# Expert 0's first chunk: low parts on GpSimd from a copy in SBUF, and a routing group's temporaries moved to PSUM

## The chip, the core and the metric

The kernel runs on one core of a Trainium2 chip. The metric is the device time of one execution in microseconds (us). A core has five instruction queues that matter here: PE (the matrix unit TensorE), DVE (VectorE), ACT (ScalarE), POOL (GpSimd) and SP (SyncE, which here only issues transfers). Each works through its own instructions in order and waits on semaphores for the others.

## The reference, cut to what matters

A linear attention with a decaying state makes `x` (3072 tokens of 384 numbers), and a mixture of 8 experts with two chosen per token works on it:

```python
logits = x @ w_gate
noise_scale = np.log1p(np.exp(x @ w_noise))
noisy_logits = logits + noise_scale * noise
top2 = np.argpartition(-noisy_logits, 2, axis=1)[:, :2]
...
for e in range(E):
    for k in range(2):
        mask = top2[:, k] == e
        h = np.maximum(x[mask] @ w1[e], 0.0)
        out[mask] += top2_w[mask, k, None] * (h @ w2[e])
```

`w1[e]` is 384 by 1024, `w2[e]` is 1024 by 384, everything is float32.

## The kernel before, in words

**Attention, then experts.** The tokens come in 24 blocks of 128. A loop over the blocks does the attention, stores each block of `x` to a scratch array `xd` in device memory, and computes the logits. The blocks form two routing groups, 0 to 11 and 12 to 23. When a group's logits are there, `route(g)` finds the two best experts of each token, counts with matmuls how many earlier tokens chose the same expert, and so gives each token a place in its expert's list. `drop` makes 0/1 matrices out of the places, and `place` multiplies them on PE, so that the token numbers land at their places in a list `L`. `rows` turns `L` into row numbers `GR`, and POOL gathers the rows from `xd` by indirect transfers (`xgather`).

**Experts in chunks.** An expert has up to 832 tokens, in a chunk of 3 tiles of 128 tokens and a chunk of 3 such tiles and one of 64. `p1(e, ci)` is the first product of a chunk: for each of 8 blocks `f` of the hidden size it makes a PSUM tile `ph` with 9 matmuls. `p2(e, ci)` is the second product: for each tile of tokens 24 matmuls into a PSUM tile `pym`. Both split every float32 factor into a high part (rounded to fp32r, a shorter format) and a low part (the rest), and add three products: high by high, high by low, low by high. So behind each `ph` the activations are needed twice: ACT writes the high part of `relu(ph)` into `hb[:, f, 0]`, and DVE writes `max(ph, 0)` minus the high part into `hb[:, f, 1]`. `p2` takes the blocks `f` in order, and of each the high part twice and then the low part.

**Routing among the products.** Group 0 is routed while the attention runs. Group 1 is complete only when the attention ends, and the whole of the list for expert 0's second chunk depends on it. So its `route(1)` is a generator, of which `rstep` takes some steps at each point of `p1(0, 0)` (after each of the 8 blocks, each time with a credit of `STEPS_P1`) and of `p2(0, 0)` (every fourth matmul). The instructions of both stand mixed in DVE's queue in that order. Two points bind PE to it. The counting matmuls (L842 to L848, into the PSUM bank `RT`) need the one-hot matrix `r_om` of DVE (L834). And `place` (L728) needs the 0/1 matrices, which DVE makes (L706, L711, L714) and ACT scales (L719). A finished `drop` waits in `late_mm` with a count of steps, 2, until its matmuls are issued.

**Temporaries.** In group 0 `route` keeps its temporaries in free columns of the PSUM bank `RT` (`own` is true); in group 1 it keeps them in `PS`, a tile in SBUF. In the first case the gates are stored to `xd` by the branch at L870 to L890, in the second by that at L899 to L908.

**Buffers.** `stg` is a pool of 3 SBUF tiles through which the weights come in. Expert 0's weights are split before `p1(0, 0)`; expert 1's first loads go through `stg` after `p2(0, 0)`.

Of the kernel before, what the change touches and what calls it, by code (L numbers as in the profile page):

```python
# [9 lines left out]
F32 = mybir.dt.float32  # L10
# [5 lines left out]
AF = mybir.ActivationFunctionType  # L16
# [13 lines left out]
FILL = 1  # L30
PVB = 4
CV_EARLY = 3
STEPS_P1 = 1.15
STEPS_P2 = 4.2
STEPS_R = 1.6
STEPS_L0 = 0.9
# [21 lines left out]
def kernel(  # L58
# [14 lines left out]
    nc = tc.nc  # L73
    B, H, S, D = r.shape
    N, E = noise.shape
# [18 lines left out]
    NJ = NM + 1  # L94
    XW = DM + E
    GROUPS = ((0, 12), (12, 24))
    GB = max(b - a for a, b in GROUPS)
# [517 lines left out]


    RT = psum.tile([128, 512], F32, name="RT", tag="rt")
    PS = rtp[0].tile([128, 4 * GB * E], F32, name="PS", bufs=1)
    PG = [RT]

    def P(k, shape):
# [66 lines left out]
    def drop(g, mm2, ej2, ijv, w_, c0, first):  # L688

        i0, i1 = GROUPS[g]  # L690
        wp_ = w_ + w_ % 2
        o = 5 * GB * E + E
        o = o if o + 2 * wp_ <= 512 else 0
        pL = RT[:, o:o + 2 * wp_].rearrange("p (a b) -> p a b", a=2)
        c = 0.1 + 0.004 * wp_
        n = GD
        parts = []
        while late_mm:
            yield "hold"
        for j0 in range(0, i1 - i0, n):  # L700
            js = slice(j0, j0 + n)
            oa = rtp[0].tile([128, n, 128], BF16, name="r_oa", bufs=2)
            ob = rtp[0].tile([128, n, 2 * E * NJ], BF16, name="r_ob", bufs=2)[:, :, :2 * wp_].rearrange(
                "p n (a b) -> p n a b", a=2)
            sh = [128, n, 64, 2]
            nc.vector.tensor_tensor(oa.rearrange("p n (a b) -> p n a b", b=2), mm2[:, js, None, :].to_broadcast(sh),  # L706
                                    im[:, None].to_broadcast(sh), op=ALU.is_equal)
            yield 0.45
            sh = [128, n, wp_ // 2, 2]
            o0, o1 = (ob[:, :, a].rearrange("p n (a b) -> p n a b", b=2) for a in range(2))  # L710
            nc.vector.tensor_tensor(o1, ej2[:, js, None, :].to_broadcast(sh),  # L711
                                    ijv.rearrange("p (a b) -> p a b", b=2)[:, None].to_broadcast(sh), op=ALU.is_equal)
            yield c
            nc.vector.tensor_mul(o0, o1, thi[:, i0 + j0:i0 + j0 + n, None, :].to_broadcast(sh))  # L714
            yield c
            parts.append((oa, ob))
            yield 0.05
        late_mm.append([2, lambda: place(n, parts, pL),
                        lambda: [nc.scalar.activation(ob[:, :, 1], ob[:, :, 1], AF.Copy, scale=pcol) for _, ob in parts],  # L719
                        lambda: placed(pL, w_, c0, first), False])  # L720

    late_mm = []

    def place(n, parts, pL):
        m = len(parts) * n
        for j in range(m):
            oa, ob = parts[j // n]
            nc.tensor.matmul(pL.rearrange("p a b -> p (a b)"), oa[:, j % n, :],  # L728
                             ob[:, j % n].rearrange("p a b -> p (a b)"), start=(j == 0), stop=(j == m - 1))
# [20 lines left out]
    def route(g, lists=True, behind=iter(())):  # L750
        i0, i1 = GROUPS[g]
        n = i1 - i0
# [2 lines left out]
        sh = [128, n, E]  # L755
        T = T_of(n)

        PG[0] = PS if lists and g == len(GROUPS) - 1 else RT
        if g:
            while lists and late_mm and g < len(GROUPS) - 1:  # L760
                yield "hold"
# [405 lines left out]
    def p1(e, ci, mid=lambda: None):  # L1167
# [8 lines left out]
        for f in range(NF):  # L1176
# [8 lines left out]
            for j, (a, x, d) in enumerate(q):  # L1185
                nc.tensor.matmul(ph[:, :w_], a[:, d, fs], x[:, d, :w_], start=(j == 0), stop=(j == len(q) - 1))  # L1186
                if j == 4:
                    mid()
            for h_, a, b in parts:
                nc.scalar.activation(h_[:, f, 0, :], ph[:, a:b], AF.Relu)  # L1190
            for h_, a, b in parts:
# [334 lines left out]
    for s in range(1, len(seq)):  # L1526
        e, ci = seq[s]
# [188 lines left out]
```

## Time and profile before

| what | value |
|---|---|
| runs, median of 3 | 588.56 us (586.28 to 589.39) |
| profiled execution, its own time | 585.73 us |
| its span, first to last instruction | 583.7 us |
| PE busy | 565.8 us, 97% of the span |
| DVE, ACT, POOL busy | 343.4, 283.9, 281.2 us |
| mean granted clock of TensorE | 0.998 of full speed |

The span is a little shorter than the execution's own time, which also holds what lies before the first and behind the last instruction. The median of the runs is 2.83 us above the profiled execution. Durations below come from that one execution.

### The profile page before, as it was taken

Reading aid. Unit: us, or ns where it says so; the run is one execution under the profiler, and the core shown is the slowest. Engines: PE = TensorE matmul, PEld = TensorE weight load, DVE = VectorE, ACT = ScalarE, POOL = GpSimd, SP = SyncE. Lnnn points to the kernel's source line nnn. Section 1 sums busy time; section 2 is a strip of 40 time slices with the busy share of each in tenths; the row PEclk is TensorE's granted clock in tenths of the full one; section 3 lists DMA queues with packets and bytes.
Section 4 is the critical chain, followed back from the end, with each engine's and each line's share of the span. In section 5 each row is a group of like instructions: output and inputs, shape, how many; then the busy total and the mean of one; then the engine's idle time right before and its main releaser. Section 6 shows DMA issues by size and latency. Waiting matters only on the chain.

```text
span 583.7 us, 13848 instructions
## 1 busy us (share of the span) xinstructions
PE 565.8 (97%) x5351; PEld 540.9 (93%) x5352; DVE 343.4 (59%) x788; ACT 283.9 (49%) x714; POOL 281.2 (48%) x420
## 2 busy tenths in 40 slices
PE   8999898999999999999999999999999999999995
PEld 5899897989989999999999999999999999999995
DVE  7898796898772744545455554545363556454331
ACT  4348786842553525455444554544545455445220
POOL 8998776911445532354433453535162455333322
PEclk9999999999999999999999999999999999999999
DMA  8988998476515725566456738455646556433111
GB/s 162 200 196 189 221 233 196 130 210 192 156 34 177 230 88 148 156 155 188 111 179 101 189 101 204 135 166 152 142 128 144 167 134 179 111 97 99 54 35 42
DMA packets 143289, 86.53 MB, mean 148 GB/s; under 512 B 118688, under 2 KB 133279, under 8 KB 143216
## 3 DMA queue, kind: packets, MB, share of 16 engines
q1 hardware_dynamic: 132432, 56.76, 40.4%
q0 software_dynamic: 10160, 28.81, 16.6%
q8 instruction: 44, 0.72, 0.5%
q14 instruction: 29, 0.24, 0.1%
q10 hardware_dynamic: 624, 0.00, 0.1%
HBM read 58.81 MB, written 19.86 MB: 135 GB/s over the span
## 4 chain that ended last, share of the span: by engine, by line
PE 84%; POOL 5%; DMA 3%; DVE 2%; issue 2%; SPq 2%; ACT 1%; POOLq 0%; DVEq 0%; ACTq 0%
PE ph L1186 37%; PE pym L1222 34%; PE py L535 3%; DMA kt<-in_k_dram 3%; PE pym L1215 2%; PE pym L1213 2%; POOL rku L414 2%; POOL kd L406 2%; PE PAB L480 2%; SPq L158 1%; POOL rku L418 1%; PE KX L228 1%; PE py L577 1%; PE py L437 1%; PE RT L728 1%
## 5 line engine op out<-in xcount | busy, mean ns | idle before, releaser
L1222 PE MATMUL pym<-w1h,hb 128*128 128x384 f32 x768 | 200.4, 337 | 0.0
L1222 PEld LDWEIGHTS pym<-w1h,hb 128*128 128x128 f32 x768 | 139.4, 188 | 0.2
L1192 DVE SCALAR_TENSOR_TENSOR hb<-ph,hb 128x384 fp32r<-128x384 f32 x128 | 71.0, 556 | 115.4 <-ACT ht L1190 74.5
L1186 PE MATMUL ph<-xh,w0h 128*128 128x384 f32 (+1 forms) x384 | 135.5, 353 | 0.0
L1186 PE MATMUL ph<-xh,w0l 128*128 128x384 f32 (+1 forms) x384 | 135.2, 352 | 0.0
L1186 PE MATMUL ph<-xl,w0h 128*128 128x384 f32 (+1 forms) x384 | 129.9, 352 | 0.0
L1222 PE MATMUL pym<-w1l,hb 128*128 128x384 f32 x384 | 129.3, 337 | 0.0
L1190 ACT ACTIVATE hb<-ph 128x384 fp32r<-128x384 f32 x128 | 62.7, 491 | 105.1 <-PE ph L1186 102.2
L1247 POOL DMA_INDIRECT out_dram<-ot,TK x56 | 60.5, 1081 | 100.1 <-DVE ot L1241 42.8
L1075 POOL DMA_INDIRECT xg<-xd,GR x56 | 60.1, 1073 | 48.7 <-DVE r_e L611 25.3
L1186 PEld LDWEIGHTS ph<-xh,w0h 128*128 128x128 f32 x384 | 72.2, 188 | 3.7 <-issue 0.2
L1186 PEld LDWEIGHTS ph<-xh,w0l 128*128 128x128 f32 x384 | 72.2, 188 | 3.1
L1186 PEld LDWEIGHTS ph<-xl,w0h 128*128 128x128 f32 x384 | 71.9, 188 | 3.3
L1090 POOL DMA_INDIRECT pv<-out_dram,GA x49 | 50.4, 1028 | 51.0 <-DMA out_dram<-ot,TK 38.6
L1222 PEld LDWEIGHTS pym<-w1l,hb 128*128 128x128 f32 x384 | 72.2, 188 | 0.1
L1160 ACT ACTIVATE xh<-xj 128x384 fp32r<-128x384 f32 (+1 forms) x42 | 21.1, 502 | 43.4 <-DVE xj L1158 43.2
L1230 ACT ACTIVATE ot<-pym 128x384 f32<-128x384 f32 x42 | 20.4, 486 | 39.7 <-PE pym L1222 32.8
L1161 DVE TENSOR_TENSOR xl<-xj,xh 128x384 fp32r<-128x384 f32 (+1 forms) x42 | 22.5, 535 | 24.8 <-ACT xh L1160 24.8
L1146 ACT ACTIVATE pl<-xg 128x768 uint16<-128x768 uint16 (+1 forms) x42 | 35.3, 841 | 2.8 <-DMA xd<-pl 2.8
L488 DVE TENSOR_TENSOR am<-PAB,mneg 128x512 int32<-128x512 int32 x48 | 30.8, 684 | 3.7 <-PE PAB L480 3.2
L457 ACT ACTIVATE cv<-vt,c 128x48 f32<-128x48 f32 x120 | 30.2, 324 | 0.2
L406 POOL TENSOR_TENSOR kd<-kt,tabk 128x192 f32<-128x192 f32 x46 | 28.3, 635 | 3.9 <-DMA kt<-in_k_dram 3.5
(309 smaller groups left out, 821.2 us busy)
## 6 DMA issues: line engine op xcount, KB each, us to landing
stg<-in_moe_w_dram SPq DMA_DIRECT2D x24, 512.0 KB, 4.7
stg<-in_moe_w_dram SPq DMA_DIRECT2D x32, 384.0 KB, 3.7
xd<-x SPq DMA_DIRECT2D x24, 196.0 KB, 3.2
rd<-in_r_dram SPq DMA_DIRECT2D x24, 192.0 KB, 4.3
vt<-in_v_dram SPq DMA_DIRECT2D x24, 192.0 KB, 3.7
out_dram<-ot SPq DMA_DIRECT2D x16, 288.0 KB, 4.2
kt<-in_k_dram SPq DMA_DIRECT2D x23, 192.0 KB, 4.2
xg<-xd,GR POOLq DMA_INDIRECT x56, 3.1
```

Source lines behind the costliest of these rows:

```text
L406: nc.gpsimd.tensor_mul(KD[i][:, h], kt[i][:, h], tabk[:, h, :D])
L457: nc.scalar.activation(CV[i][:, h, :], vt[i][:, h, :], AF.Copy, scale=C8[i][:, h, :])
L488: nc.vector.tensor_tensor(am[:, :, h].bitcast(I32), pa[:, :, h].bitcast(I32), mneg[:, None].to_broadcast([128, 2, NP // 2, 128]), op=ALU.b ...
L1075: nc.gpsimd.indirect_dma_start(out=xg[:n, :XW if e else DM], out_offset=None, in_=xd[:rows_of(early_)], in_offset=bass.IndirectOffsetOnAxi ...
L1090: nc.gpsimd.indirect_dma_start(out=pv[:n], out_offset=None, in_=out, in_offset=bass.IndirectOffsetOnAxis(ap=GA[:n, e * NJ + t:e * NJ + t + ...
L1146: nc.scalar.activation(pl[:n], XG[e, t][:n, :DM].bitcast(U16).rearrange("p (d two) -> p two d", two=2), AF.Copy)
L1161: nc.vector.tensor_sub(xl, xj, xh.bitcast(F32))
L1186: nc.tensor.matmul(ph[:, :w_], a[:, d, fs], x[:, d, :w_], start=(j == 0), stop=(j == len(q) - 1))
L1190: nc.scalar.activation(h_[:, f, 0, :], ph[:, a:b], AF.Relu)
L1192: nc.vector.scalar_tensor_tensor(h_[:, f, 1, :], ph[:, a:b], 0.0, h_[:, f, 0, :].bitcast(F32), op0=ALU.max, op1=ALU.subtract)
L1222: nc.tensor.matmul(py, hb[:, f, a, hs], x[:, f, :], start=(j == 0), stop=(j == len(q) - 1))
L1247: st = nc.gpsimd.indirect_dma_start(out=out, out_offset=bass.IndirectOffsetOnAxis(ap=TK[:n, q:q + 1], axis=0), in_=ot[:n], in_offset=None, ...
```

## The change

Four edits. In `p1` of the first chunk of expert 0 only, ACT writes `relu(ph)` as float32 into a tile of the pool `stg` (L1189 of the changed kernel), a second ACT instruction rounds this copy into the high part, and POOL, no longer DVE, subtracts to get the low part. Group 1's temporaries lie in the columns of `RT`, as group 0's do, and `PS` is gone. `STEPS_P1` is 1.65 in place of 1.15. And the first list of group 1 waits 3 steps in place of 2 before its `place` is issued.

```diff
-STEPS_P1 = 1.15
+STEPS_P1 = 1.65
...
-    PS = rtp[0].tile([128, 4 * GB * E], F32, name="PS", bufs=1)
...
-        late_mm.append([2, lambda: place(n, parts, pL),
+        late_mm.append([3 if first is False and w_ == NJ else 2, lambda: place(n, parts, pL),
...
-        PG[0] = PS if lists and g == len(GROUPS) - 1 else RT
...
+            if (e, ci) == seq[0]:
+                ht32 = stg.tile([128, 1024], F32, name="stg")[:, :wb]
+                nc.scalar.activation(ht32, ph[:, :wb], AF.Relu)
+                nc.scalar.activation(hb[:, f, 0, :], ht32, AF.Copy)
+                nc.gpsimd.tensor_sub(hb[:, f, 1, :], ht32, hb[:, f, 0, :].bitcast(F32))
+                yield
+                continue
```

Line numbers of the changed kernel differ: from `P` to `route` they are 1 less, from there to `p1` 2 less, and behind the new lines 5 more.

The first place is PE in `p1(0, 0)`, where the counting matmuls of group 1 start. Before, they stand behind the last of the 72 matmuls into `ph`:

```order
L1186 MATMUL ph<-xh,w0h_891 128x384
L1186 MATMUL ph<-xl,w0h_891 128x384
L1186 MATMUL ph<-xh,w0l_892 128x384
L842 LDWEIGHTS ltri
L842 MATMUL RT<-r_om,ltri 128x96 [waits DVE_49]
L844 LDWEIGHTS ones_b
L844 MATMUL RT<-r_om,ones_b 128x88
```

In the changed kernel these rows stand behind the 54th matmul into `ph`, that is behind block 5 of 0 to 7:

```order
L1184 MATMUL ph<-xh,w0h_890 128x384
L1184 MATMUL ph<-xl,w0h_890 128x384
L1184 MATMUL ph<-xh,w0l_891 128x384
L840 LDWEIGHTS ltri
L840 MATMUL RT<-r_om,ltri 128x96 [waits DVE_49]
L842 LDWEIGHTS ones_b
L842 MATMUL RT<-r_om,ones_b 128x88
```

The 13 counting matmuls and their wait for DVE moved 18 matmuls forward.

The second place is PE at the first list's `place` in `p2(0, 0)`. Before, it stands behind the 20th matmul into `pym`:

```order
L1222 MATMUL pym<-w1h_1660,hb 128x384
L1222 MATMUL pym<-w1h_1660,hb 128x384 [waits Activation_49]
L1222 MATMUL pym<-w1l_1661,hb 128x384
L728 LDWEIGHTS r_oa [waits DVE_49]
L728 MATMUL RT<-r_ob,r_oa 128x16 [waits Activation_49]
L728 LDWEIGHTS r_oa
L728 MATMUL RT<-r_ob,r_oa 128x16
```

In the changed kernel it stands behind the 8th, and the low parts before it wait for POOL:

```order
L1227 MATMUL pym<-w1h_1659,hb 128x384 [waits Pool_49]
L1227 MATMUL pym<-w1h_1659,hb 128x384
L1227 MATMUL pym<-w1l_1660,hb 128x384
L727 LDWEIGHTS r_oa [waits DVE_49]
L727 MATMUL RT<-r_ob,r_oa 128x16 [waits Activation_49]
L727 LDWEIGHTS r_oa
L727 MATMUL RT<-r_ob,r_oa 128x16
```

`place` moved 12 matmuls forward within `p2`.

The third place is DVE in the middle of `p1(0, 0)`, in `route(1)`. Before, the low parts (L1192) stand among the routing steps:

```order
L779 RECIPROCAL r1r<-PS 128x96 [waits DVE_49]
L781 TENSOR_TENSOR r_s<-r_nl,r1r 128x96 [waits DVE_49]
L783 TENSOR_TENSOR r_s_3033<-r_s 128x96 [waits DVE_49]
L784 SCALAR_TENSOR_TENSOR r_sn<-r_s,nz 128x96
L1192 SCALAR_TENSOR_TENSOR hb<-ph,hb 128x384 [waits Activation_49]
L786 TENSOR_SCALAR PS<-r_s_3033 128x96 [waits DVE_49]
```

In the changed kernel they are gone from DVE, and `RT` stands for `PS`:

```order
L777 RECIPROCAL RT<-RT 128x96 [waits DVE_49]
L779 TENSOR_TENSOR r_s<-r_nl,RT 128x96 [waits DVE_49]
L781 TENSOR_TENSOR r_s_3019<-r_s 128x96 [waits DVE_49]
L782 SCALAR_TENSOR_TENSOR r_sn<-r_s,nz 128x96
L784 TENSOR_SCALAR RT<-r_s_3019 128x96 [waits DVE_49]
```

DVE loses 8 such instructions, 6 of them ahead of `r_om`, and POOL has 8 new ones, in front of the four gathers of the list that `place` fills.

## Rows read from the trace of the kernel before

**Rows 1.** The page's chain that ended last: shares by engine, then by line.

```profile
PE 84%; POOL 5%; DMA 3%; DVE 2%; issue 2%; SPq 2%; ACT 1%; POOLq 0%; DVEq 0%; ACTq 0%
```

**Rows 2.** Stretches: length; busy us (xcount) of PE, PEld, DVE, ACT, POOL; clock; DMA.

```profile
124.60:137.60 13.00, 13.00 (x83) 12.85 (x82) 12.24 (x46) 3.71 (x9) 0.00 (x0) 1.00 0.99 303
137.60:143.00 5.40, 4.49 (x45) 4.18 (x42) 4.45 (x24) 1.08 (x3) 0.00 (x0) 1.00 0.48 156
```

**Rows 3.** PE's instructions in order of time: start us, duration us.

```profile
124.86 0.34 PE L1186 MATMUL ph<-xh,w0l 128*128 128x384 f32 x1
...
137.15 0.33 PE L1186 MATMUL ph<-xh,w0l 128*128 128x384 f32 x1
137.32 0.22 PE L842 MATMUL RT<-r_om,ltri 128*128 128x96 bf16 x1
...
137.76 0.42 PE L1222 MATMUL pym<-w1h,hb 128*128 128x384 f32 x1
...
141.96 0.29 PE L728 MATMUL RT<-r_ob,r_oa 128*128 128x16 bf16 x6 [0.43 <-ACT r_ob L719]
142.74 0.29 PE L728 MATMUL RT<-r_ob,r_oa 128*128 128x16 bf16 x6 [0.49 <-ACT r_ob L719]
```

**Rows 4.** PE, the same view, at a later list's matmuls in `p1(0, 1)`.

```profile
161.18 0.36 PE L1186 MATMUL ph<-xl,w0h 128*128 128x448 f32 x1
161.64 0.86 PE L728 MATMUL RT<-r_ob,r_oa 128*128 128x100 bf16 x12
```

**Rows 5.** DVE's instructions in order of time, in `p1(0, 0)` and behind it.

```profile
125.39 0.25 DVE L763 SCALAR_TENSOR_TENSOR PS<-lg 128x96 f32<-128x96 f32 x1
125.92 0.26 DVE L766 SCALAR_TENSOR_TENSOR PS<-lg,nz 128x96 f32<-128x96 f32 x1
...
136.12 0.55 DVE L1192 SCALAR_TENSOR_TENSOR hb<-ph,hb 128x384 fp32r<-128x384 f32 x1
136.59 0.16 DVE L827 TENSOR_SCALAR r_da<-r_da 128x12 f32<-128x12 f32 x1
136.66 0.20 DVE L834 TENSOR_TENSOR r_om<-OH 128x96 bf16<-128x96 bf16 x1
...
138.51 0.16 DVE L599 TENSOR_SCALAR r2t<-r_da 128x12 f32<-128x12 f32 x1
...
142.14 0.18 DVE L714 TENSOR_TENSOR r_ob<-r_ob,thi 128x48 bf16<-128x48 bf16 x1
```

**Rows 6.** Groups of instructions with their shapes: busy us, mean ns of one, idle before.

```profile
L599 DVE TENSOR_SCALAR PS<-r_a 128x96 f32<-128x96 f32 x1 | 0.2, 204 | 0.0
L599 DVE TENSOR_SCALAR RT<-r_a 128x96 f32<-128x96 f32 x1 | 0.3, 260 | 0.0
...
L358 POOL TENSOR_TENSOR w1l<-stg,w1h 128x384 fp32r<-128x384 f32 x2 | 2.0, 1008 | 0.0
...
L1190 ACT ACTIVATE hb<-ph 128x384 fp32r<-128x384 f32 x128 | 62.7, 491 | 105.1 <-PE ph L1186 102.2 <-DVE mx L1057 1.9 <-DVE PS L611 1.0
...
L1160 ACT ACTIVATE xh<-xj 128x384 fp32r<-128x384 f32 x36 | 18.9, 525 | 32.0 <-DVE xj L1158 31.9
...
L719 ACT ACTIVATE r_ob<-r_ob,pcol 128x48 bf16<-128x48 bf16 x4 | 1.2, 326 | 4.0 <-DVE r_ob L714 4.0
```

**Rows 7.** DVE in order of time, in the attention, while POOL computes.

```profile
72.04 0.82 DVE L766 SCALAR_TENSOR_TENSOR RT<-lg,nz 128x96 f32<-128x96 f32 x1
...
113.35 0.52 DVE L940 TENSOR_SCALAR GR<-lt 128x3 int32<-128x3 f32 x1
```

**Rows 8.** POOL in order of time, at the same two moments, and its gathers after `p1(0, 0)`.

```profile
72.01 1.42 POOL L425 TENSOR_TENSOR rku<-rT,kT 128x256 f32<-128x256 f32 x2 [1.35 <-DVE r_a L765]
...
112.70 1.15 POOL L414 TENSOR_TENSOR rku<-rd,kt 128x192 f32<-128x192 f32 x2
...
144.12 0.94 POOL L1075 DMA_INDIRECT xg<-xd,GR  x1 [25.33 <-DVE r_e L611]
```

**Rows 9.** Later execution of the same DVE line, with POOL idle.

```profile
143.68 0.17 DVE L940 TENSOR_SCALAR GR<-lt 128x4 int32<-128x4 f32 x1
```

## The prediction

> **What bounds the kernel now.** First the chain that ended last: PE is 84% of it [rows 1], and PE is busy 565.8 of the 583.7 us of the span, so time can only come from the few places where PE stands still. The change touches the stretch from 124.6 us on, where expert 0's first products begin, so I read the busy time by stretch next. In the first product PE works all 13.00 us, DVE 12.24 of them, POOL none. Right behind it PE works only 4.49 of 5.40 us [rows 2]. PE's own order of time shows where: in front of the two halves of the list's `place` it waits 0.43 and 0.49 us for ACT's scaling [rows 3], together 0.92 us. The same kind of wait returns twice, smaller, in `p1(0, 1)`: the matmul at 161.18 should be followed after some 0.20 us, and the `place` begins at 161.64 [rows 4], so 0.26 us; its second half waits some 0.16 more by the same reading, and the other one (at 168.17) is alike. That is 2 x 0.42 = 0.84 us. All waits of PE on the routing of group 1 are thus 0.92 + 0.84 = **1.76 us**, and the change can win no more than that: everything else in this stretch is matmuls, whose number it doesn't alter. The counting matmuls cost no wait before: the last `ph` matmul starts at 137.15, they at 137.32, the first of `p2` at 137.76 [rows 3].
>
> **The change, part by part.** I work out when each of the two meeting points of PE and DVE comes now.
>
> *PE's side of the comparison.* The 72 matmuls into `ph` go from 124.86 (the second) to 137.15, that is 12.29 us for 70 steps, 0.1756 us each [rows 3]. The counting matmuls now stand behind the 54th, so PE asks for `r_om` at 124.86 + 53 x 0.1756 = 134.17 us.
>
> *DVE's side.* Before, `route(1)` starts at 125.39 and `r_om` is done at 136.66 + 0.20 = 136.86 [rows 5]. Six of the eight low parts lay ahead of it. The last of them starts at 136.12 and the next instruction at 136.59, 0.47 us later [rows 5]; since they overlap with the end of the one before, I take 0.37 each, 2.2 us for six (2.8 at 0.47). That gives 134.66. The temporaries in PSUM cost a little: the same instruction took 260 ns on `RT` and 204 ns on `PS` [rows 6]; some seven of the chain are of this kind, 0.35 us. So `r_om` comes at about 135.0 us (134.4 to 135.0 by the two values for a low part), and PE, which waited nowhere here, now **waits 0.85 us** (0.25 to 0.85). The steps were sped up by more than DVE was relieved. Queued behind that wait on PE are the last 18 matmuls of the first product and all of `p2`.
>
> *The port.* POOL was idle here [rows 2]; now it subtracts 8 times. A subtraction of this shape took 1008 ns on POOL [rows 6], and one comes every 9 x 0.1756 = 1.58 us, so POOL is busy 64% of the time. The trace shows what that does to DVE: L766, which reads `lg` and `nz`, both in SBUF, took 0.26 us with POOL idle (at 125.92) [rows 5], but 0.82 us at 72.04 [rows 7], while the first of two POOL multiplications of 0.71 us each ran from 72.01 [rows 8]. And L940 took 0.52 us at 113.35 [rows 7], beside the second half of 1.15 us of POOL work from 112.70 [rows 8], and 0.17 us with POOL idle [rows 9]. DVE ends when POOL's instruction ends. The Trainium skill ("SBUF — State Buffer", section "Who interferes with whom") says it as a rule: a DVE instruction with two SBUF inputs (or one in a two-port mode, which single-input ones can have) and a GpSimd instruction that reads SBUF exclude each other, and the one that comes second waits for the whole of the other; the trace agrees with its 0.82 us. By that rule the move of the temporaries takes most of `route(1)` out of reach, and only a few instructions are left.
>
> Those with both inputs in SBUF are, ahead of `r_om`, L783 with L784 and L816 (squares, noise, the difference of the maxima), and behind it L857, two L706 and two L714. Each may lose nothing or up to 1.0 us. Block k's subtraction begins when PE's nine matmuls, ACT's relu of 491 ns and ACT's copy of 525 ns [rows 6] are done: the third (k = 2) ends on PE at 124.86 + 26 x 0.1756 = 129.4, so it runs from about 130.7 to 131.7. L783 comes by my chain at 130.9, into it: 0.7 us late. L816 then comes at 135.3, between two subtractions. I take 0.65 of the 0 to 2.0 us that the two could lose together, so the wait at the comparison becomes **1.5 us** in all (0.25 to 2.85).
>
> *The place.* From the end of the counting matmuls, PE has 18 x 0.1756 + 8 x 0.1756 = 4.57 us of matmuls up to `place`, and some 0.25 more to its second half. DVE needed from L599 at 138.51 to the end of the second L714 at 142.14 + 0.18, 3.81 us [rows 5], then ACT, which is now behind relu and copy of block 7 (3.16 + 0.49 + 0.53 + two scalings of 326 ns that overlap a little [rows 6]: 4.8 us). Without the port PE would wait for nothing. With it, the first L714 comes (at 2.95) during block 6's subtraction (2.7 to 3.7) and the second (at 4.5) during block 7's (4.3 to 5.3): ACT is done at some 5.9, a wait of 1.1 us. I take **1.0 us**, near the upper end, since the trace shows the port at work (0 to 1.3), against 0.92 before.
>
> *The later lists.* The one issued in the middle of a block of `p1(0, 1)` keeps its 0.42 us, since ACT has just got that block's relu in front of the scalings. The three others stand between tiles; by the same sums they lose 0 to 0.3 each. I take 0.64, against 0.84.
>
> *What costs nothing.* ACT's 8 copies (525 ns [rows 6]) lie under PE's 1.58 us a block; ACT was busy 3.71 of 13.00 us [rows 2]. The last low part, 5.3 us behind the counting matmuls at the latest, is used by PE at 18 + 8 + 15 matmuls, 7.2 us, plus the `place`: 2 us to spare; without this cover each block's subtraction would cost its 1.0 us. POOL's queue: the four gathers of the second chunk stand behind the 8 subtractions. They began at 144.12 after 25.33 us of idling [rows 8], and will begin within 1 us of that, since `place` comes at the same time by the sums above; the subtractions are over by some 142. The loads of expert 1's weights on SP wait for the last subtractions in `stg`, and are issued long after. The gates' store of the other branch still stands on SP behind the same 16 zero stores and waits for the gathers.
>
> *Sum.* 1.5 (new wait) + (1.0 - 0.92) + (0.64 - 0.84) = **+1.4 us**. From there to the end PE works without a gap that could take it in. Against the profiled 585.73 us that makes 587.1; against the median of the runs, which is 2.83 us above it, 588.56 + 1.4 = **590.0 us**.
>
> **The rivals.**
>
> *The steps fit: a gain.* DVE's relief could be larger than 0.37 a low part and the two-input instructions fall between subtractions. Then the comparison waits 0.25, the place 0, and the later lists 0.42: 0.67 against 1.76, so -1.1 us, 587.5. For it: DVE 12.24 of 13.00 busy [rows 2], so it was the limit of the routing. Against it: PE asks 137.32 - 134.17 = 3.15 us earlier, `r_om` had 0.46 to spare [rows 3, 5], and six low parts give back 2.2.
>
> *The port decides: slower by more than 0.5%.* Both exposed instructions ahead of `r_om` lose a whole subtraction (0.85 + 2.0 = 2.85), and the five behind it hold the place up by 2.0: 2.85 + (2.0 - 0.92) - 0.2 = +3.7 us, 592.3. It decides from 3.2 us of blocking in all. For it: DVE's 0.82 us [rows 7]. Against it: with POOL at 64%, half a subtraction is what a blocked one loses on average. By the rule of the Trainium skill ("SBUF — State Buffer", above) blocks of these sizes happen, as in my forecast; it would not by itself make all seven whole.
>
> *The change moves the wait and nothing else.* Without any effect of the port the comparison waits 0.85, the place 0, the later lists 0.64: 1.49 against 1.76, -0.3 us, 588.3.
>
> **How the numbers follow.** Chances: my forecast 0.50 (its own range, with the port's two terms at nothing and at their largest short of the rival, 588.3 to 592), wait moved only 0.20, gain 0.16, port decides 0.10, something else late, POOL's low parts for instance, 0.04. Three runs of before lie 3.1 us apart, about 0.5%, which is what a measurement of this kernel can tell from no change; so the forecast, the moved wait and the gain all lie inside 0.5% (2.9 us), and even the whole 1.76 us would. Faster by over 0.5%: 0.05, for the runs' scatter; slower: 0.12, from the port and the rest; the same: 0.83. The range runs from the gain less half a microsecond of scatter, 587.0, to the port's rival, 592.3.
>
> **What will show it.** In the changed profile: a wait of PE in front of the counting matmuls for DVE of 0.25 to 2.9 us (none: the DVE sum is wrong); DVE's L783, L816 and L714 at 0.3 to 1 us, far above the 0.26 of such an instruction with POOL idle (unchanged: the port is no term); the wait at `place` about as long as before or gone; POOL's subtractions at about 1.0 us; the gathers within 1 us of 144. The forecast would be wrong if POOL's subtractions took over 1.58 us each, so that they fall behind PE, or if a transfer of the second chunk came late for PE's transposes.

## The result, and the profile after

The changed kernel takes 593.91 us (median of 13 runs, 590.62 to 596.48), the kernel before 586.49 in 13 runs on the same chip: a ratio of 1.0112 [1.0091, 1.0133]. That is slower by more than 0.5%, 1.6 us above the upper end of the predicted range. An execution more than 1.5% above the fastest of its kernel counts as slow, and all ratios here are of the others, while the medians hold every execution. The profiled execution has a span of 588.9 us (its own time 590.62) against 583.7 (585.73).

The chain that ended last, shares by engine; DVE had 2% before [rows 1]:

```profile
PE 83%; DVE 6%; SPq 3%; POOL 3%; DMA 2%; issue 2%; ACT 1%; POOLq 0%; DVEq 0%; ACTq 0%
```

PE in order of time (start us, duration us; in brackets the idle time before the instruction and what ended it), where [rows 3, 4] stood:

```profile
125.55 0.44 PE L1184 MATMUL ph<-xh,w0h 128*128 128x384 f32 x1
...
134.99 0.34 PE L1184 MATMUL ph<-xh,w0l 128*128 128x384 f32 x1
137.48 0.20 PE L840 MATMUL RT<-r_om,ltri 128*128 128x96 bf16 x1 [2.15 <-DVE RT L835]
...
139.24 0.52 PE L1184 MATMUL ph<-xh,w0h 128*128 128x384 f32 x1
...
142.69 0.34 PE L1227 MATMUL pym<-w1h,hb 128*128 128x384 f32 x1
...
144.27 0.52 PE L727 MATMUL RT<-r_ob,r_oa 128*128 128x16 bf16 x12
...
159.33 0.47 PE L1184 MATMUL ph<-xh,w0h 128*128 128x448 f32 x1 [0.42 <-ACT xh L1103]
...
161.47 0.43 PE L727 MATMUL RT<-r_ob,r_oa 128*128 128x100 bf16 x6 [0.59 <-ACT r_ob L718]
```

PE waits 2.15 us for the counts, and not for `r_om` (L830) but for the line behind it, L835. The `place` at 144.27 waits for nothing. The matmul at 139.24 takes 0.52 us where that at 134.99 took 0.34. The stretches around it say why (busy us of PE, PEld, DVE, ACT, POOL; granted clock; DMA share; GB/s):

```profile
135.00:137.40 2.40, 0.33 (x2) 0.10 (x2) 2.12 (x10) 1.01 (x2) 1.81 (x2) 1.00 0.93 295
137.40:139.00 1.60, 1.52 (x20) 1.52 (x20) 0.84 (x8) 0.00 (x0) 0.14 (x1) 0.93 1.00 317
139.00:142.00 3.00, 3.00 (x11) 3.00 (x10) 2.72 (x14) 1.01 (x2) 0.38 (x1) 0.50 0.79 254
142.00:143.00 1.00, 1.00 (x6) 1.00 (x6) 0.93 (x4) 0.05 (x1) 0.62 (x1) 0.90 0.00 0
```

After the idle gap PE came back and was granted 0.50 of its clock (1.2 instead of 2.4 GHz) for about 3 us, though it was busy throughout. The 18 matmuls left of the first product, from 137.90 to 142.69 by PE's order of time, took 4.79 us; at the pitch of [rows 3] they take 18 x 0.1756 = 3.16. That is 1.6 us which stood in no term of the prediction.

DVE in order of time, where [rows 5] stood:

```profile
126.36 0.26 DVE L761 SCALAR_TENSOR_TENSOR RT<-lg 128x96 f32<-128x96 f32 x1
...
132.09 0.77 DVE L781 TENSOR_TENSOR r_s<-r_s 128x96 f32<-128x96 f32 x1
...
136.81 0.25 DVE L830 TENSOR_TENSOR r_om<-RT,r_m 128x96 bf16<-128x96 f32 x1
137.09 0.33 DVE L835 TENSOR_REDUCE RT<-r_om 128x8 f32<-128x96 bf16 x1
...
141.91 0.76 DVE L713 TENSOR_TENSOR r_ob<-r_ob,thi 128x48 bf16<-128x48 bf16 x1
...
155.75 0.36 DVE L658 TENSOR_TENSOR r_os<-OH,SLF 128x192 f32<-128x192 bf16 x1 [1.51 <-DMA xd<-r_os]
```

POOL in the same stretch (compare [rows 8]):

```profile
131.74 1.01 POOL L1191 TENSOR_TENSOR hb<-stg,hb 128x384 fp32r<-128x384 f32 x1 [0.57 <-ACT hb L1190]
...
145.88 0.96 POOL L1073 DMA_INDIRECT xg<-xd,GR  x1 [0.81 <-DVE r_os L658]
```

The port shows as predicted, with two late instructions: L781 (0.77 us, against 0.26 for the same step before, its L783) ends with the subtraction that runs from 131.74, and one L713 takes 0.76 against 0.18 [rows 5]. The gathers begin 1.8 us later than before, 1.0 of which is the later start of the whole stretch. A new wait that was not predicted is at 155.75: DVE needs `r_os` again while the gates' store still reads it.

From the first matmul into `ph` of expert 0 to that of expert 1 the stage takes 193.03 - 125.55 = 67.48 us, against 188.04 - 124.58 = 63.46 before. From there to the end both kernels take 395.7 to 395.9. So 4.0 us of the span's 5.2 are lost in the stage: 2.15 (counts) + 1.63 (clock) + 0.18 (other spacing in the first product) + 0.35 + 0.08 (second chunk) - 0.37 (from there to the second chunk: no wait at the place, but a new one of 0.42 for ACT's `xh`). The remaining 1 us lies before 125.55, in the attention, where the change has no instruction.

### The profile page after: what moved, and what is told of

Same layout as the page of the kernel before. It is cut to its first block, busy times and chain, and to the rows that moved or that the text cites. A ratio compares the mean times of both kernels' runs of the same rounds, so it can differ in the third digit from the quotient of the medians.

```text
span 588.9 us, 13872 instructions
## 1 busy us (share of the span) xinstructions
PE 568.1 (96%) x5351; PEld 542.9 (92%) x5352; DVE 345.2 (59%) x783; ACT 288.4 (49%) x722; POOL 286.9 (49%) x428
## 4 chain that ended last, share of the span: by engine, by line
PE 83%; DVE 6%; SPq 3%; POOL 3%; DMA 2%; issue 2%; ACT 1%; POOLq 0%; DVEq 0%; ACTq 0%
PE ph L1184 35%; PE pym L1227 33%; PE py L535 4%; SPq L158 2%; PE PAB L480 2%; PE pym L1220 2%; PE pym L1218 2%; DMA kt<-in_k_dram 2%; PE KX L228 1%; PE py L577 1%; POOL rku L414 1%; PE py L437 1%; PE RV L498 1%; POOL rku L418 1%; POOL kd L406 1%
## 5 line engine op out<-in xcount | busy, mean ns | idle before, releaser
L1197 DVE SCALAR_TENSOR_TENSOR hb<-ph,hb 128x384 fp32r<-128x384 f32 x120 | 66.8, 556 | 113.2 <-ACT ht L1195 72.0
L1195 ACT ACTIVATE hb<-ph 128x384 fp32r<-128x384 f32 x120 | 59.0, 491 | 95.9 <-PE ph L1184 95.6
L1088 POOL DMA_INDIRECT pv<-out_dram,GA x49 | 49.1, 1003 | 49.6 <-DMA out_dram<-ot,TK 37.2
L1158 ACT ACTIVATE xh<-xj 128x384 fp32r<-128x384 f32 (+1 forms) x42 | 21.1, 502 | 44.4 <-DVE xj L1156 44.0
```

What stands on the lines that cost most here:

```text
L1088: nc.gpsimd.indirect_dma_start(out=pv[:n], out_offset=None, in_=out, in_offset=bass.IndirectOffsetOnAxis(ap=GA[:n, e * NJ + t:e * NJ + t + ...
L1197: nc.vector.scalar_tensor_tensor(h_[:, f, 1, :], ph[:, a:b], 0.0, h_[:, f, 0, :].bitcast(F32), op0=ALU.max, op1=ALU.subtract)
```

## The experiments

Each ran in 5 rounds beside the kernel before. The kernels of one set shared a chip, and the medians of before in the four sets were 585.8, 589.8, 586.8 and 589.5 us, so the ratios are to be compared and not the times. "Stage" is the length just defined, from the profile; kernels whose instructions are those of before gave 63.5, 64.3 and 64.3, those of the changed kernel 67.5, 68.6, 68.3 and 68.3, so it is good to about 1 us.

| kernel | median | ratio to before | stage |
|---|---|---|---|
| e1: 1.55 steps | 593.94 | 1.0110 [1.0058, 1.0162] | 67.8 |
| e2: filler matmuls in the gap | 593.29 | 1.0130 [1.0080, 1.0179] | 68.6 |
| e3: 1.15 steps | 592.08 | 1.0104 [1.0067, 1.0141] | 65.8 |
| e4: before, 1.65 steps | 589.48 | 1.0042 [1.0014, 1.0069] | 65.9 |
| e5: changed, old addresses | 592.96 | 1.0065 [1.0028, 1.0102] | 68.3 |
| e6: before, 32 bytes lower | 588.90 | 0.9971 [0.9941, 1.0002] | 64.3 |
| e7: only the low parts on POOL | 595.14 | 1.0080 [1.0046, 1.0113] | 70.9 |
| e8: changed, 32 bytes lower | 592.35 | 1.0058 [1.0024, 1.0092] | 68.3 |
| e9: gates out of `RT`, 1.15 | 585.90 | 0.9984 [0.9955, 1.0013] | 62.1 |
| e10: gates out, 1.35 | 589.20 | 1.0035 [1.0010, 1.0060] | 65.0 |
| e11: temporaries in PSUM, no work on POOL | 591.22 | 1.0071 [1.0041, 1.0100] | 66.4 |
| e12: gates out, 1.65 | 587.95 | 1.0034 [1.0007, 1.0062] | 65.2 |
| e13: before, moved addresses | 593.25 | 1.0062 [1.0027, 1.0098] | 64.3 |
| e14: the changed kernel again | 595.61 | 1.0104 [1.0069, 1.0138] | 68.6 |
| e15: gates out, 1.65, old addresses | 592.52 | 1.0045 [1.0005, 1.0085] | 67.3 |
| e16: gates out, 1.15, old addresses | 588.68 | 0.9986 [0.9950, 1.0021] | 63.7 |

### First set: the steps and the clock

e1 and e3 set `STEPS_P1` of the changed kernel to 1.55 and 1.15, e4 sets that of the kernel before to 1.65, and e2 adds work for PE, whose result nobody uses, ahead of the counting matmuls:

```diff
+        if g and lists:
+            pf = psr[0].tile([128, 384], F32, name="pfill", tag="py1")
+            for _ in range(13):
+                nc.tensor.matmul(pf..., wsrc, wsrc..., start=True, stop=True)
```

e1: 

> The changed kernel with STEPS_P1 at 1.55: the counting matmuls stand behind the 63rd matmul into ph instead of the 54th, nearly all else is as in the change. Theory A (PE waits too early at the comparison, and after that wait TensorE's clock falls): PE asks 9 x 0.1756 = 1.6 us later, so the wait of 2.15 us shrinks to about 0.6 us, the granted clock stays at 1.00 in the following stretch, and the time falls by 1.6 + 1.6 = some 3 us against the changed kernel. Theory B (POOL's subtractions block DVE, and the loss is theirs): the wait is still there with its lost 0.5 us, the time falls by 1.6 us at most and the low clock may stay.

e2: 

> The changed kernel with 13 matmuls of zeros (128x384, bf16) into an unused PSUM bank in front of the counting matmuls: PE still waits for DVE until the same moment, but works for about 2 us of that time. Theory A: no gap of over 0.3 us in PE, the granted clock stays at 1.00 afterwards, and the 18 matmuls into ph take 3.2 us in place of 4.8; the time falls by 1.6 us, and the rest of the loss stays. If the low clock has nothing to do with the gap in PE (power, say), it comes back and the time is that of the changed kernel. Theory B gives no gain either.

e3: 

> The changed kernel with STEPS_P1 back at 1.15: low parts on POOL, temporaries in PSUM, a wait of 3 steps, but the counting matmuls stand behind the 72nd matmul into ph, as before. Theory A: no wait at the comparison, no low clock, the place stands later so that its wait is small too: 1 us faster to 1 us slower than the kernel before. Theory B: the port still blocks DVE, so it is 2 us or more slower than before.

e4: 

> The kernel before with STEPS_P1 at 1.65 alone: low parts stay on DVE, temporaries in SBUF, POOL idle. PE's request for r_om moves forward and DVE is not relieved. Theory A: the wait at the comparison is longer than in the changed kernel, by the six low parts of 0.37 us about 4 us if the place of the matmuls is the same, and the clock falls after it: 6 to 9 us slower than before. Theory B (the port): nothing of it can appear, as POOL is idle, so the time is within 2 us of the kernel before.

The view is PE's order of time, for e1, e2, e3 and e4 in turn:

```profile
144.28 0.20 PE L840 MATMUL RT<-r_om,ltri 128*128 128x96 bf16 x1 [0.57 <-DVE RT L835]
...
150.83 0.46 PE L727 MATMUL RT<-r_ob,r_oa 128*128 128x16 bf16 x12 [2.18 <-DVE RT L611]
```

```profile
144.41 0.48 PE L727 MATMUL RT<-r_ob,r_oa 128*128 128x16 bf16 x12 [2.05 <-DVE RT L611]
```

```profile
145.49 0.46 PE L727 MATMUL RT<-r_ob,r_oa 128*128 128x16 bf16 x12 [1.78 <-DVE RT L611]
```

```profile
133.67 0.20 PE L842 MATMUL RT<-r_om,ltri 128*128 128x96 bf16 x1 [1.09 <-DVE r_om L834]
```

With fewer steps the wait for the counts shrinks to 0.57 us (e1) or goes (e3), as expected, but nothing is won: a wait of about 2 us now stands at the `place`, and the last that it waits for is L611. That is a step of the gates, which `place` doesn't use. In the changed kernel this wait was hidden behind the slow clock. With fillers in the gap the clock stayed at 1.00, and the first product took 15.60 us instead of 17.14, so in this place the idle gap is what brought the slow clock. But the place's wait of 2.05 us then brought it again. Stretches of e2:

```profile
135.00:140.00 5.00, 4.98 (x41) 4.04 (x40) 3.86 (x21) 1.50 (x3) 1.61 (x2) 1.00 1.00 313
140.00:145.00 5.00, 2.95 (x27) 2.63 (x26) 4.15 (x14) 2.10 (x5) 2.01 (x2) 0.95 0.18 56
145.00:150.00 5.00, 5.00 (x22) 5.00 (x23) 4.80 (x26) 0.73 (x2) 3.11 (x4) 0.71 0.27 79
```

e4's miss says that the steps alone cost 0.4%, not the 6 to 9 us expected: `r_om` came 11.5 us after the first matmul (12.3 before), since only four low parts stood ahead of it, and PE waited 1.09 us for it, not 4. So the first theory, waits of PE for the comparison and the clock behind them, explained the changed kernel's trace and not what undoing it gives.

Why does `place` wait for the gates? In e3 PE asks at 143.71 (145.49 - 1.78). ACT has scaled the list's second half at 144.65, and PE starts only when the four L611 are over (ACT, then DVE in order of time):

```profile
144.32 0.33 ACT L718 ACTIVATE r_ob<-r_ob,pcol 128x48 bf16<-128x48 bf16 x1 [0.47 <-DVE r_ob L713]
```

```profile
140.17 1.02 DVE L855 TENSOR_TENSOR ie_n<-ie_n,r_s 128x1 f32<-128x1 f32 x1
...
144.61 0.82 DVE L611 SCALAR_TENSOR_TENSOR RT<-RT,r2r 128x12 f32<-128x12 f32 x4
```

The gates' temporaries stand in the same PSUM tile `RT` as the sum that `place` writes, in other columns. The program makes PE's matmul into a tile wait for all that DVE did on that tile before it.

But the wait has two parts, and the gates are only one of them. Until 144.65 the list itself was late: L855 is the port again (both inputs in SBUF, 1.02 us instead of 0.16). Only the 0.84 us from there to 145.49 are the gates'. In e1, e2 and e11 (below) ACT is done at 150.00, 143.58 and 143.21 and PE starts at 150.83, 144.41 and 144.03, so the gates hold it for at least 0.82 or 0.83 us, and the list for up to 1.35, 1.2 and 0.3 us (PE could have begun the list's first half earlier). In e2 the port held both L713, which took 0.18 us before (DVE, then ACT):

```profile
140.76 0.90 DVE L713 TENSOR_TENSOR r_ob<-r_ob,thi 128x48 bf16<-128x48 bf16 x1
...
142.28 0.93 DVE L713 TENSOR_TENSOR r_ob<-r_ob,thi 128x48 bf16<-128x48 bf16 x1
```

```profile
143.25 0.33 ACT L718 ACTIVATE r_ob<-r_ob,pcol 128x48 bf16<-128x48 bf16 x1 [0.92 <-DVE r_ob L713]
```

### Second set: addresses, and the low parts alone

Without the tile `PS` and the smaller SBUF tiles that group 1 no longer needs, the attention's tiles lie 1824 bytes a partition higher. e5 and e8 add an unused tile of 1824 and of 32 bytes to the changed kernel, e6 one of 32 bytes to the attention's pool of the kernel before. e7 is the kernel before with the block of new lines in `p1` and nothing else.

```diff
+    rtp[0].tile([128, 456], F32, name="pad", bufs=1)
     PG = [RT]
```

e5: 

> The changed kernel with an unused tile of 1824 bytes a partition at the place where the temporaries' tile stood, so that the attention's tiles have the addresses that they had before; all else as in the change. Theory C (part of the loss is the attention phase, whose loads run slower at the new addresses): the first loads are issued and land as before (third row of SP near 5.2 us with 0.9 us, not 6.7 with 1.1; kt in use near 10.2 and not 11.5), the DMA share of the first 20 us falls from 1.06 to 0.90, the first product begins at 122 to 124.6 instead of 125.55, and the median falls from 593.9 by 1 to 3.5 us, to 590.4 to 592.9; the stage's own loss of 4.0 us stays. Theory A (all of the loss is PE's waits for the counts and the place and the clock that falls behind them): the median stays at 593 to 594.5 and the first product begins at 125 to 126.

e6: 

> The kernel before with one unused tile of 32 bytes a partition in the attention's pool, which moves the tiles that the loads write and the stores read by 32 bytes; not one instruction is changed. Theory C, in the form that it is the place within 64 bytes that counts (before: multiples of 64; after: 32 off): slower than before by 1 to 3.5 us, 587.5 to 590, with the loads' rows of SP near 6.7 us and the DMA share of the first 20 us at 1.06. Theory C in the form that it is where the 1824 bytes moved the tiles to: as before, 586.5. Theory A: as before, 586.5, first product at 122 to 124.6.

e7: 

> The kernel before with only the activations' low parts of the first product moved to GpSimd from a copy in SBUF (temporaries in their own tile, 1.15 steps). Theory A (the waits come from the temporaries in PSUM and the later counts): no wait of PE for the counts, none over 1 us at the place, the clock stays at 1.00, 585.5 to 587. Theory B (DVE's instructions that read two SBUF tiles are held up by GpSimd's subtractions): two such rows 0.5 to 0.6 us longer than before, PE waits 1 to 2 us more at the place or for the activations, 587.5 to 588.5. Theory C has no part in it: addresses are those of before.

e8: 

> The changed kernel with an unused tile of 32 bytes a partition, which puts the attention's tiles back on multiples of 64 bytes, 1792 bytes from where they were before. Theory C in the form of the place within 64 bytes: the attention phase as in the kernel with the old addresses, first product at 122 to 124.6, 590.4 to 592.9. Theory C in the other form and theory A: as after, 593 to 594.5, first product at 125 to 126.

e7 is the clearest miss. DVE is rid of eight low parts of 0.55 us, and yet `r_om` comes 14.1 us after the first matmul, where it came 12.3 after it. DVE in order of time in e7:

```profile
128.78 2.92 DVE L611 SCALAR_TENSOR_TENSOR PS<-PS,r1r 128x96 f32<-128x96 f32 x5
...
133.94 2.53 DVE L789 SCALAR_TENSOR_TENSOR PS<-PS,r_s 128x96 f32<-128x96 f32 x4
...
137.38 0.67 DVE L808 TENSOR_TENSOR OH<-r_nl,r_m 128x96 bf16<-128x96 f32 x1
...
138.67 0.94 DVE L814 TENSOR_TENSOR OH<-r_zp,r_m 128x96 bf16<-128x96 f32 x1
```

Before, the five L611 took 1.42 us, the four L789 1.09 (without the low part among them), L808 and L814 0.26 each: 1.5 + 1.4 + 0.4 + 0.7 = 4.0 us of blocking. As long as the temporaries are in SBUF, nearly every step has two SBUF inputs. In the changed kernel the same five L611 on `RT` took 1.47 us beside the same subtractions. So the move to PSUM is what takes this blocking away (the chain up to `r_om` took 13.3 us here, 10.7 in the changed kernel). The whole time doesn't tell the two apart: e7 is at 1.0080, e5, with the move and 1.65 steps, at 1.0065. And e7's stage of 70.9 us holds more than blocking: PE waited 1.20 us for the counts and 2.61 us at a later list, where the clock fell to 0.50 for about 3 us.

e6 takes away the form of the address theory that looks at 64 bytes. e5 and e8 came out nearer to the kernel before than the changed kernel had (1.0065 and 1.0058 against 1.0112), with first products that began no earlier (126.21 and 125.15): inconclusive, and therefore the fourth set.

### Third set: the gates out of the shared tile

e9, e10 and e12 (1.15, 1.35 and 1.65 steps) are the changed kernel with the gates' temporaries and the counts `sm` of group 1 in SBUF tiles of their own, as before; the rest of `route(1)` stays in `RT`. With that the gates are stored by the other branch, from `r_a`.

```diff
+        if g and own:
+            e2, et = T("e2", [128, n]), None
...
-        sm = V(5 * GB * E + E + 2 * E, [128, E, 1]) if own else ...
+        sm = V(5 * GB * E + E + 2 * E, [128, E, 1]) if own and not g else ...
...
-            if own:
+            if own and not g:
                 gp = V(4 * GB * E + 2 * GB, [128, 2, n])
```

e11 is the changed kernel with the low parts back on DVE and 1.15 steps; against the kernel before it has the temporaries in PSUM, the wait of 3 steps and the new addresses.

e9: 

> The changed kernel with 1.15 steps, and with the gates' temporaries and the counts of group 1 kept in SBUF as before, so that DVE's gate steps no longer touch the PSUM tile into which PE's place writes. Theory A' (PE's matmuls into the shared tile wait for every earlier DVE instruction on that tile, needed or not): no wait for the counts; the wait of 1.8 us at the place for the gates' L611, which the kernel with 1.15 steps alone had, falls to 0.5 us or less, the one of 1.1 us behind it too; the stage from the first product of expert 0 to that of expert 1 takes 64.0 to 64.8 us instead of 65.8; 589 to 590.5. Rival (the place waits for the list's own numbers, which GpSimd's subtractions hold up): the place still waits 1 to 1.8 us, now for ACT's scaling; 591.5 to 593.

e10: 

> As the one before with 1.35 steps (counts behind the 63rd matmul of the first product, place behind the 16th of the second). Theory A': a wait of 0 to 0.6 us for the counts and of 0 to 0.5 us at the place, no fall of the clock behind them, stage 63.5 to 64.5 us, 588 to 590. Rival: place waits 1.5 us or more, the clock falls behind it, 592 to 594.

e11: 

> The kernel before with only the temporaries of group 1 in PSUM (low parts on DVE, 1.15 steps). Reading of the two profiles so far: the temporaries cost DVE's chain 1.5 us in small instructions, against 11.5 us before, so the counts come at 12.3 + 1.5 us and PE waits 1.2 to 1.7 us for them, then at the place up to 1.8 us for the gates by theory A'; the port has no part, GpSimd stands idle. 588.5 to 590.5. Rival (the temporaries in PSUM are free, only the low parts on GpSimd cost): as before, 586 to 587.

e12: 

> The changed kernel, 1.65 steps, with the gates' temporaries and the counts of group 1 in SBUF. Theory A': PE waits for the comparison alone, 1.7 to 1.8 us instead of 2.15; if the clock falls behind it as in the changed kernel, the first product takes 16.5 to 17 us and the median is 592 to 593.5; if the shorter wait doesn't bring the fall, 15.3 us and 590 to 591. Rival (the wait for the counts isn't from the shared tile): 2.15 us as in the changed kernel, 593 to 594.5.

PE in order of time in e9: the counts and the place, neither with a wait, nor has any other matmul from 126.6 to 188.7 one over 0.15 us.

```profile
139.32 0.22 PE L842 MATMUL RT<-r_om,ltri 128*128 128x96 bf16 x1
...
144.01 0.46 PE L727 MATMUL RT<-r_ob,r_oa 128*128 128x16 bf16 x12
```

And DVE in e9 at that moment:

```profile
143.71 0.78 DVE L611 SCALAR_TENSOR_TENSOR r_e<-r_e,r2r 128x12 f32<-128x12 f32 x4
```

The place runs from 144.01 while the same four L611 run until 144.49. The stage takes 62.1 us, and the ratio falls from e3's 1.0104 to 0.9984. Not all of that is the gates': the list was not late here (the step that took 1.02 us in e3 took 0.16), and the attention's tiles lie elsewhere (fourth set). e9 is the version without waits; e16, with the same instructions, has three at later lists (0.37 to 0.68 us) and a stage of 63.7 us, as long as before. e9's interval still holds 1, so it is no measured gain: the 1.76 us that all of group 1's waits cost before are about what can be told from nothing. e12 confirms the part at the counts: the wait is 1.78 us, now for `r_om` itself, and the clock behind it stays at 1.00:

```profile
136.80 0.20 PE L842 MATMUL RT<-r_om,ltri 128*128 128x96 bf16 x1 [1.78 <-DVE r_om L832]
```

```profile
138.00:140.00 2.00, 2.00 (x13) 2.00 (x13) 1.79 (x10) 0.82 (x2) 0.00 (x0) 1.00 1.02 328
```

At 587.95 us it came out better than the 590 to 591 expected with the clock up, as e9 did (585.9, where 589 to 590.5 was expected): the expectations had no part for the addresses, which these kernels also change (fourth set). e10 is within its expectation of time, with seven small waits of 0.2 to 0.6 us; its stage of 65.0 us is above the 63.5 to 64.5 expected. e11 shows the shared tile without POOL's work. Its 591.2 us lie above the 588.5 to 590.5 expected, but for the counts PE waits only 0.18 us (1.2 to 1.7 expected). With POOL idle and the same six low parts, DVE's chain took 137.55 - 125.25 = 12.30 us, against 11.47 before [rows 5], so the temporaries in PSUM cost it 0.83 us and not the 1.5 of the expectation (DVE in order of time):

```profile
125.25 0.26 DVE L761 SCALAR_TENSOR_TENSOR RT<-lg 128x96 f32<-128x96 f32 x1
...
137.30 0.25 DVE L830 TENSOR_TENSOR r_om<-RT,r_m 128x96 bf16<-128x96 f32 x1
```

Two waits of PE stand behind it:

```profile
144.03 0.47 PE L727 MATMUL RT<-r_ob,r_oa 128*128 128x16 bf16 x12 [1.14 <-DVE RT L611]
...
158.70 0.87 PE L1184 MATMUL ph<-xl,w0h 128*128 128x448 f32 x3 [1.61 <-DVE xl L1104]
```

The Trainium skill ("PSUM — Partial Sum Buffer", section "PSUM bank collisions raise a hardware error") says to guard PSUM with semaphores by bank and quadrant (32 of a bank's partitions), not by address, since two engines in one bank and quadrant at once raise an error whatever columns they touch. The waits in the traces agree with a program that keeps to it (the error itself no run here shows). Taking the waits away is no way out then; temporaries in another place are.

### Fourth set: the addresses again

e13 is the kernel before with an unused tile of 224 bytes at the end of the attention's pool. This puts every one of its tiles exactly 2048 bytes below its place in the changed kernel. e14 is the changed kernel beside it. e15 and e16 are e12 and e9 with an unused tile of 1664 bytes that gives the tiles their old places.

```diff
+    att.tile([128, 56], F32, name="pad", bufs=1)
     att_stack.close()
```

e13: 

> The kernel before with an unused tile of 224 bytes a partition at the end of the attention's pool, so that each of the attention's tiles stands exactly 2048 bytes below its place in the changed kernel; not one instruction is changed. Theory C (the new addresses slow the loads, and that costs time): the DMA engines move 134 GB/s in the first 10 us instead of 153, their share of the first 20 us is 1.05 to 1.16 instead of 0.90, and the median is 1 to 3.5 us above that of the kernel before in the same call. Rival (the transfers are slower but hidden): the same shares, the median within 1 us of the kernel before. Second rival (the place within 2048 bytes isn't what counts): shares as before.

e14: 

> The changed kernel as it is, beside the others on the same chip, as the point that they are compared with. All theories: 1.006 to 1.013 times the kernel before; PE waits 2.1 to 2.2 us for the counts and the clock falls behind that wait.

e15: 

> The changed kernel, 1.65 steps, with the gates' temporaries and the counts of group 1 in SBUF, and an unused tile of 1664 bytes that puts the attention's tiles back to where they stood before. Theory C: 1 to 2 us faster than the same kernel without that tile, which was 1.0034 times the kernel before: 0.999 to 1.002. Rival (addresses cost nothing): 1.002 to 1.005.

e16: 

> The same with 1.15 steps, whose stage took 62.1 us against 63.5 before and had no wait of PE over 0.15 us. Theory A' alone: 0.9955 to 1.0013 times the kernel before as without the tile, near 0.998. Theory C in addition: 0.994 to 0.998.

e13 has the instructions of the kernel before, and is slower than it by 0.62% [0.27, 0.98]; the medians lie 3.8 us apart, a little more than the 1 to 3.5 expected. The first 10 us of before, the changed kernel, e13 and e5 (columns as above):

```profile
0.00:10.00 10.00, 8.02 (x80) 4.74 (x83) 6.12 (x22) 5.74 (x12) 8.42 (x43) 1.00 0.83 153
```

```profile
0.00:10.00 10.00, 8.56 (x74) 4.79 (x76) 6.16 (x21) 5.63 (x12) 8.05 (x43) 1.00 1.05 134
```

```profile
0.00:10.00 10.00, 7.91 (x77) 4.67 (x79) 6.27 (x21) 5.74 (x12) 8.10 (x43) 1.00 1.05 135
```

```profile
0.00:10.00 10.00, 8.60 (x66) 4.84 (x67) 5.63 (x21) 5.25 (x12) 7.93 (x42) 1.00 0.84 158
```

The DMA engines are busier and move less wherever the tiles stand at the new places. The loads show it one by one (issues of the first 10 us: KB each, median us to landing; before, then changed):

```profile
rd<-in_r_dram SPq DMA_DIRECT2D x3, 192.0 KB, 3.7
```

```profile
rd<-in_r_dram SPq DMA_DIRECT2D x3, 192.0 KB, 4.8
```

And DVE's last step on the third block of `x` begins at 20.84 before, at 21.99 in the changed kernel and 21.98 in e13 (rows of L564). In the 15 profiles not named so far it is the same: 21.8 to 22.2 in the other five kernels at the new place, 20.3 to 21.1 in seven at the old one or 32 bytes from it, 21.1 to 21.3 in e9, e10 and e12, whose tiles lie at a third place. So some 1.2 us are lost early in the attention. After that the executions differ by more than this among themselves: they begin the first product at 122 to 133 us, with granted clocks down to 0.66 in single stretches of the attention.

The pieces that a load writes into the tiles of `r` are 192 bytes, 256 bytes apart. In the four layouts that ran, they begin at 64 (before), 32 (e6), 192 (e9, e10, e12) and 96 (changed, e13) within 256 bytes. In the first two a piece stays inside a block of 256 bytes, in the others it crosses into the next. The DMA share of the first 10 us was 0.83, 0.83, 0.99 and 1.05. The Trainium skill ("DMA: Bandwidth & Descriptors", section "How a descriptor splits into AXI transactions") says that a descriptor is split into transactions of at most 256 bytes, and that a read of one must start at a multiple of 256. It says this of reads, while what moved here is where the pieces are written; the order of the four layouts would fit the same on that side. Against it speaks that the tiles of `v`, and those of `k` behind the first, have no padding: their pieces stand 192 bytes apart, so half of them cross at 64 and 192 and three quarters at 32 and 96, and yet the share was the same at 64 and 32. That the crossing is the cause is argued from four layouts, not tested by itself. e15 and e16 gained nothing over e12 and e9 (1.0045 to 1.0034, 0.9986 to 0.9984), so at the place of 192 no loss shows; only at 96, with loads of 4.8 us, was one measured.

## Why the prediction was wrong

The sum of +1.4 us failed at three steps. It counted a wait of PE as its length, and the slow clock behind it stood in no term (1.6 us). It held a matmul to wait for its own operands alone, and a PSUM temporary to cost next to nothing, so the new wait was 2.15 us instead of 1.5. And it had no term for the loads, whose tiles moved (about 0.45%).

Of the loss of 1.1%, the old addresses give back about 0.45% (1.0104 and 1.0112 for the changed kernel, 1.0065 and 1.0058 for e5 and e8), which agrees with e13's 0.62% [0.27, 0.98]. The gates out of `RT` give 0.1 to 0.2% more (e15, 1.0045), and the steps back at 1.15 the last 0.6% (e16, 0.9986). The intervals are as wide as some of these steps. The first and the last are shown by two kernels each; that the gates matter is shown by e3 against e9, 1.0104 against 0.9984, which also holds the addresses' part. As far as these intervals tell, steps and shared tile work together: 1.15 steps win nothing while the gates are in `RT` (e3), and the gates cost little at 1.65 steps, where the slow clock covers them.

**The comparison (predicted 1.5 us, measured 2.15).** PE asked when it was said to, behind the 54th matmul. A low part gave back what was predicted: with six of them the chain took 12.30 us in e11, without them 10.70 in the changed kernel, of which 0.52 are the port's, so (12.30 - 10.18) / 6 = 0.35 us each, against the 0.37 taken. The port took these 0.52 from one instruction instead of the 0.65 from two. The term that was mis-sized is "the temporaries in PSUM cost a little": 0.35 us from one pair of rows, 0.83 in e11. And PE was taken to wait for `r_om` alone, while the counts also wait for L835, done 0.36 us after it; without L835 the wait was 1.78 (e12).

**The clock behind that wait (not predicted, 1.6 us).** The prediction counted a wait as its length; behind this one 18 matmuls took 4.79 us instead of 3.16, and with the gap filled (e2) they did not.

**The place (predicted 1.0, measured 0).** It was 0 only because PE was slow. Where PE was not (e1, e2, e3) it waited 1.8 to 2.2, above the bound of 1.3. The list's own part was sized rightly: in e2, with the same steps, it is up to 1.2 us, and from the port, as forecast. The step that failed was to look only for what the place needs (the list's numbers) and not at what shares its tile, at least 0.83 us more.

**What costs nothing.** PE waited for none of ACT's copies, POOL's gathers and the last subtractions, though two of these came later than said: the subtractions were over at 145.06, not by 142, and the gathers began at 145.88, not within 1 us of 144. The gates' store was judged by its place on SP alone: its source `r_os` is needed again, and DVE waited 1.51 us for it. In the later lists PE waits 0.59 us in this profile (0.64 predicted), but 1.6, 1.2 and 1.3 us in e14, e5 and e8, so that agreement is luck.

**What was left out.** "Everything else in this stretch is matmuls" was true of the stretch. But taking away tiles moved 24 blocks' worth of loads, and that was no term at all. At about 0.45% it stands beside the 0.6% that e5 and e8 still lose without it.

**The rivals.** "The port decides" gave the nearest time (592.3) for the wrong reason: two blocks of 0.5 to 0.6 us in the changed kernel. It blocks DVE for longer only without the move to PSUM (e7). "The steps fit" is nearest in e9 and e16, which have other steps and other tiles and no wait for the counts or the first `place`; its gain of 1.1 us isn't shown there (62.1 and 63.7 us in the stage against 63.5 to 64.3, ratios whose intervals hold 1).

Open: the medians of the changed kernel lie 7.4 us above those of before, the profiled executions 4.9. The fall of the clock in the stage can't be the reason: it is in the profiled 4.9 already. The address loss is larger in the medians, too (3.8 us in e13), than the 1.2 us that its loads lose early in the attention. In the fourth set the timed executions of e13, which has no fall in the stage, have a median granted clock of 0.991, those of before 0.994; by an estimate from these two, 0.003 of 593 us or 1.8 us of its loss is time at the lower clock. Whether the later loads bring it, no run here tells.

## What to carry to other kernels

When a temporary moves into PSUM, list who else uses that tile. In this program each matmul into it waited for the last access of DVE ahead of it, needed or not, so a late helper chain (here the gates) belongs elsewhere. When a tile goes away, look at what moves: run the old kernel once with the new addresses before the new instructions are blamed. And price a wait of PE with the clock that may follow, by a profile with something in the gap.

## What was not expected of the hardware

- In the first products, after waits of 2.15 (changed), 2.17 (e14), 2.16 (e5), 2.15 (e8), 2.18 (e1), 2.05 (e2) and 2.61 us (e7), PE was granted 0.50 of its clock for about 3 us, beginning as the wait ended or up to 1.5 us behind it, when PE was busy again. After 1.77 and 1.84 (e15) and 1.78 us (e3, e12) it stayed at 1.00. But the length of a wait doesn't decide it alone. In the attention PE stayed at 1.00 after 2.25 us (e2) and 2.19 us (e10), and fell after 1.87 us (e9). The rows of e2 and then of e9, PE's matmul behind the wait and the stretch behind it:

```profile
64.28 0.40 PE L228 MATMUL KX<-ident,x 64*128 64x64 f32 x6 [2.25 <-DVE x L564]
```

```profile
64.20:70.00 5.80, 5.62 (x138) 5.24 (x138) 4.43 (x9) 4.91 (x18) 4.04 (x6) 1.00 1.12 256
```

```profile
63.22 0.53 PE L228 MATMUL KX<-ident,x 64*128 64x64 f32 x6 [1.87 <-DVE x L564]
```

```profile
63.30:66.80 3.50, 3.50 (x62) 3.38 (x62) 2.84 (x5) 3.41 (x12) 2.98 (x5) 0.51 1.17 236
```

- The same loads of 192 KB landed after 3.7 us (before) or 4.8 us (changed), at 153 and 134 GB/s; e13, the instructions of before with the tiles at another place, moved 135 GB/s.
- With both inputs in SBUF five DVE steps took 2.92 us instead of 1.42 beside POOL's subtractions; with one of them in PSUM 1.47.
